# Spreading the last eight output transfers of an attention-and-convolution kernel over three issuing queues

## The chip, the cores and the metric

The kernel runs on one core of one Trainium2 chip. A core has five engines that run their own instruction streams: TensorE (PE in the profile) multiplies matrices into PSUM, VectorE (DVE) and ScalarE (ACT) do elementwise work, GpSimd (POOL) does slower elementwise work, and SyncE (SP) only issues transfers. The engines are held in order by semaphores. Transfers between the memory of the chip (HBM) and the on-core memory (SBUF) are issued by an instruction on SyncE, ScalarE or GpSimd and carried out by 16 DMA engines that all issuers share.

The metric is the device time of one execution in microseconds, lower is better. Before the change it is 220.62 us, the median of three runs that lie between 220.59 and 221.15 us.

## The reference

There are eight batches `b`, eight heads, 576 rows and 64 columns a head. A linear attention is followed by a gated long convolution:

```
kv  = einsum('bhsd,bhse->bhde', k, v)
out = einsum('bhsd,bhde->bhse', q, kv)
out = out / sqrt(mean(out*out, -1) + 1e-6) * g_norm
x   = out, heads side by side             # (8, 576, 512)
x1, x2, x3 = split(x @ w_proj, 3)
x2c = irfft(rfft(x2, axis=1) * rfft(filter, axis=0), axis=1)
y   = x1 * x2c * x3
return y @ w_out                          # (8, 576, 512), float32
```

The result has 9.4 MB and is written to HBM once.

## The kernel before

All work is cut into named steps, one function each, and three strings (`FIRST`, `ROUND`, `LAST`) write out by hand in which order the steps are given to the engines. `FIRST` fills the pipeline, `ROUND` is repeated seven times, each time with steps of several batches mixed, and `LAST` empties it. A step's name followed by plus or minus signs means the same step of a later or earlier batch. The Tile layer adds the semaphores and does not change the order. A step's instructions run as soon as their engine has reached them and the semaphores that they wait for are met.

A batch goes through loads by GpSimd (`L104`), the attention product and its norm, a Fourier transform written as matrix products, the gates (`L545`), the inverse transform (`L569`, `L570`), the product of the gates in `yg` (`L590`), and the last product with `w_out`. The 576 rows of a batch are held in an order of 18 blocks of 32 rows. The last product takes 128 rows at a time as one chunk; a chunk `c` has four blocks of 32, and two neighbouring chunks (0 and 1, or 2 and 3) form a pair. The 64 rows that are left over of two batches are put together in one step, `U4`.

For batches 0 to 6 a pair is one step: `U` (`L622`) multiplies, `U_ev` (`L626`) copies both chunks by ScalarE from PSUM to an SBUF tile and issues four transfers from SyncE (`L629`), each for 32 partitions and both chunks, 64 rows of 2 KB.

For the last batch the chunks are done one by one so that copies can start earlier. `V` (`L654`) multiplies one chunk, `V_ev` (`L659`) copies it by ScalarE (`va`) or VectorE (`vv`) to half of the pair's tile, and `V_out` (`L664`, steps `vd2` and `vd0`) issues the pair's four transfers, of the same 128 KB each, all from SyncE. The end of `LAST` reads

```
U4 V3 V2 vv3 ot4 V1 vv1 va2 vd2 V0 va0 vd0
```

so the pair of chunks 2 and 3 (its tile is named `o` in the trace) leaves with `vd2`, and the pair of chunks 0 and 1 (tile `rstd`) with `vd0`, which is the last work of the program. Both tiles reuse SBUF room of earlier steps. Between them stands `ot4` (`L639`, `L642`): the left-over rows of batches 6 and 7, four transfers of 64 KB; in this last batch alone they are issued from GpSimd.

Behind its last transfer SyncE waits for the landing of every transfer semaphore in use, two in one instruction, nine instructions in all (`L722`), and then all five engines meet at a barrier that ends the program. GpSimd has a drain of its own ahead of that barrier, behind its last transfer.

Of the kernel before, what the change touches and what calls it, by code (L numbers as in the profile page):

```python
# [39 lines left out]
def kernel(  # L40
# [11 lines left out]
    nc = tc.nc  # L52
# [22 lines left out]
    held, tmp = {}, {}  # L75
# [21 lines left out]
    def t_of(blk):  # L97
        return SB * (blk // 6) + blk % 6 // 3 + 2 * (blk % 3)
# [502 lines left out]
    def o_rows(b, *blks):  # L601
        t0 = [t_of(x) for x in blks]
        two = [[(t0[1] - t0[0]) * DM, 2]] if len(t0) == 2 else []
        return bass.AP(tensor=out.tensor, offset=out.offset + (b * S + t0[0]) * DM, ap=[[6 * DM, 32]] + two + [[1, DM]])
# [56 lines left out]

    def V_out(b, c0):
        for i in range(4):
            nc.sync.dma_start(out=o_rows(b, 4 * c0 + i, 4 * c0 + 4 + i), in_=tmp[c0 // 2][32 * i:32 * i + 32])  # L664

    for c in range(4):
        step["V%d" % c] = lambda b, c=c: V(b, c)
# [2 lines left out]
    for c0 in (0, 2):  # L670
        step["vd%d" % c0] = lambda b, c0=c0: V_out(b, c0)
# [55 lines left out]
```

## Time and profile before

| what | value |
|---|---|
| median of three runs | 220.62 us (220.59 to 221.15) |
| profiled execution | 221.07 us, of which the span of instructions is 219.3 us |
| PE, DVE, ACT, POOL busy | 94%, 87%, 68%, 23% of the span |
| granted TensorE clock | 0.998 |
| transfers through GpSimd's queue (q0) | 17.11 MB |
| transfers through SyncE's queue (q1) | 12.72 MB |
| transfers through a queue of ScalarE | none |

The profile page cuts the span into 40 slices of 5.5 us and gives each engine's busy share in tenths. A row of a group reads: line, engine, operation, tile written and tiles read, count, then durations. In a row of the timeline the first number is the start in us from the start of the span and the second the duration, and rows of one kind that follow each other are merged into one (x4). "SPq" is the instruction stream of SyncE; issuing does not count as busy, and the duration of a transfer row is the time that its issuer needed, not the time until the bytes arrived, which is given apart as "DMA to landing", from the start of the issue.

### The profile page before, as it was taken

The page shows a single profiled execution, that of the slowest core. Times are in us where ns is not written, and L with a number is a line of the kernel's source. Part 1 is how long each engine was busy: PE and PEld are TensorE (multiplying, and loading weights), DVE is VectorE, ACT ScalarE, POOL GpSimd, SP SyncE. Part 2 cuts the span into 40 slices and gives each one's busy share as a digit, 9 for nine tenths or more (in the row PEclk, how much of TensorE's full clock was granted, in tenths as well). Part 3 has the DMA queues.
Part 4 walks back from the last instruction along what each step waited for, and adds up shares of the span by engine and source line. Part 5 has one row for each costly group of instructions (what it writes and reads, how often), then busy time and mean ns, then how long its engine had stood idle before and what let it go on. Part 6 is the DMA issues. An engine that isn't in the chain of part 4 may idle for free.

```text
span 219.3 us, 4667 instructions
## 1 busy us (share of the span) xinstructions
PE 205.3 (94%) x1861; PEld 124.1 (57%) x1861; DVE 191.7 (87%) x323; ACT 148.6 (68%) x234; POOL 50.6 (23%) x55
## 2 busy tenths in 40 slices
PE   7599998999997999999999999999999999999970
PEld 2454635574575547754776477646774676467620
DVE  4977876899999989898989998989989999999930
ACT  3779876998954786678767785768685965542430
POOL 7843100406040206300450035000400050014030
PEclk9999999999999999999999999999999999999999
DMA  4999999988998599994969945909403211241376
GB/s 44 189 210 205 205 205 204 198 120 122 203 204 122 69 235 213 126 211 127 195 100 203 220 122 69 217 28 116 139 21 79 53 45 42 55 119 28 78 187 167
DMA packets 41064, 30.12 MB, mean 137 GB/s; under 512 B 15922, under 2 KB 36402, under 8 KB 41042
## 3 DMA queue, kind: packets, MB, share of 16 engines
q0 software_dynamic: 21200, 17.11, 51.4%
q1 hardware_dynamic: 19842, 12.72, 26.9%
q8 instruction: 14, 0.23, 0.4%
q14 instruction: 8, 0.07, 0.1%
HBM read 33.69 MB, written 9.44 MB: 197 GB/s over the span
## 4 chain that ended last, share of the span: by engine, by line
PE 74%; DMA 13%; DVE 4%; ACT 3%; issue 1%; POOL 1%; POOLq 0%; ACTq 0%
PE ps L545 23%; PE ps L622 10%; DMA kb<-in_k_dram 7%; PE ps L472 6%; PE ps L569 4%; DMA qb<-in_q_dram 3%; PE ps L321 3%; PE ps L458 3%; PE ps L479 3%; DMA qT<-qb 3%; PE ps L391 2%; PE ps L513 2%; PE ps L384 2%; PE ps L654 2%; PE ps L505 2%; PE ps L282 2%
## 5 line engine op out<-in xcount | busy, mean ns | idle before, releaser
L545 PE MATMUL ps<-x,wp 128*128 128x288 bf16 x512 | 70.4, 286 | 0.3 <-ACT x L483 0.3
L545 PEld LDWEIGHTS <-wp 128*128 128x128 bf16 x512 | 48.6, 98 | 15.3 <-issue 1.1
L526 POOL TENSOR_TENSOR Y<-tpw 97x1024 bf16<-97x1024 f32 x8 | 23.4, 2924 | 122.8 <-DVE tpw L520 85.6
L483 ACT CAST x<-ps 128x1024 bf16<-128x1024 f32 (+1 forms) x24 | 20.2, 872 | 15.5 <-PE ps L472 9.7
L405 ACT ACTIVATE rstd<-ps,bias_eps 128x576 bf16<-128x576 f32 x32 | 22.8, 740 | 6.1 <-PE ps L391 6.0
L622 PE MATMUL ps<-wo,yg 128*128 128x512 bf16 x112 | 26.5, 379 | 0.0
L551 ACT CAST x<-ps 128x576 bf16<-128x576 f32 x32 | 20.5, 643 | 7.2 <-PE ps L545 6.8
L553 DVE TENSOR_TENSOR g<-ps,x 128x576 bf16<-128x576 f32 x32 | 23.8, 750 | 0.8 <-PE ps L545 0.8
L394 ACT ACTIVATE sq<-ps 128x576 bf16<-128x576 f32 x32 | 20.3, 664 | 6.2 <-PE ps L384 5.9
L519 DVE TENSOR_TENSOR tpw<-ps,HH 97x1024 f32<-97x1024 f32 (+1 forms) x16 | 19.6, 1224 | 4.0 <-PE ps L506 2.6
L401 ACT ACTIVATE o<-ps,g_col 128x576 bf16<-128x576 f32 x28 | 20.4, 759 | 0.0
L520 DVE TENSOR_TENSOR tpw<-ps,HH 97x1024 f32<-97x1024 f32 (+1 forms) x16 | 19.4, 1215 | 0.0
L626 ACT COPY ot<-ps 128x1024 f32<-128x1024 f32 x13 | 13.3, 1021 | 8.9 <-PE ps L622 8.9
L622 PEld LDWEIGHTS <-yg 128*128 128x128 bf16 x112 | 10.6, 98 | 11.5
L569 PE MATMUL ps<-IV,Y 128*128 128x192 bf16 x128 | 16.5, 246 | 0.1
L472 PE MATMUL ps<-wp,ab 128*128 128x512 bf16 x64 | 15.1, 379 | 0.0
L573 ACT COPY os<-ps 128x576 f32<-128x576 f32 x16 | 10.3, 641 | 6.5 <-PE ps L570 6.5
L590 DVE TENSOR_TENSOR yg<-w,g 128x1152 bf16<-128x1152 bf16 x16 | 14.2, 886 | 0.0
L578 DVE TENSOR_TENSOR u<-ps,os 128x576 bf16<-128x576 f32 x16 | 12.0, 751 | 2.2 <-ACT os L573 2.2
L417 DVE TENSOR_TENSOR x<-o,rstd 128x1152 bf16<-128x1152 bf16 x16 | 11.9, 751 | 1.9 <-ACT rstd L405 1.9
L570 PE MATMUL ps<-IV,Y 97*128 97x96 bf16 x64 | 13.2, 207 | 0.0
L391 PE MATMUL ps<-sq,ind 128*128 128x288 bf16 x64 | 11.9, 286 | 0.3 <-ACT x L483 0.3
(138 smaller groups left out, 328.8 us busy)
## 6 DMA issues: line engine op xcount, KB each, us to landing
out_dram<-ot SPq DMA_DIRECT2D x52, 128.0 KB, 2.9
qb<-in_q_dram POOLq DMA_DIRECT2D x8, 576.0 KB, 8.6
kb<-in_k_dram POOLq DMA_DIRECT2D x7, 576.0 KB, 12.3
vb<-in_v_dram POOLq DMA_DIRECT2D x7, 576.0 KB, 8.8
wp<-in_moe_w_proj_dram POOLq DMA_DIRECT2D x3, 512.0 KB, 16.8
out_dram<-ot SPq DMA_DIRECT2D x12, 64.0 KB, 1.7
vb<-in_v_dram POOLq DMA_DIRECT2D x2, 288.0 KB, 7.3
kb<-in_k_dram POOLq DMA_DIRECT2D x2, 288.0 KB, 7.3
```

The source lines that it names most:

```text
L394: act.activation(out=halves(sq()[:, j]), in_=tmp['o', b, j][:, :, 0:TH], func=AF.Square)
L401: act.activation(out=by_time(osb(), j), in_=i_, func=AF.Copy, scale=g_col)
L405: act.activation(out=by_time(rstd(), j), in_=by_row(tmp['r', b, j]), func=AF.Abs_reciprocal_sqrt, scale=1.0 / D, bias=bias_eps)
L472: nc.tensor.matmul(pp[:, h], abt()[:, j, h * SB:h * SB + P], w2(j), start=(j == 0), stop=(j == NDC - 1))
L483: act.copy(out=o_(), in_=tmp[key, b])
L519: vec.tensor_mul(out=t_[:n, 0], in0=xp[:n], in1=HH[:n, g, 1:3])
L526: op(out=Yt()[:n, 2 * g:2 * g + 2], in0=t_[:n, :, 0], in1=t_[:n, :, 1])
L545: nc.tensor.matmul(pp[:, h, 0:TH], w_, x[:, j, h * TH:(h + 1) * TH], start=(j == 0), stop=(j == NDC - 1))
L551: act.copy(out=x1, in_=pp[:, :, 0:TH])
L553: vec.tensor_mul(out=halves(g13t()[:, dc]), in0=pp[:, :, 0:TH], in1=x1)
L569: nc.tensor.matmul(pp[:, i, 0:SB], Y[:, 2 * g + h, cs], IV[:, 2 * g + h, 0:SB], start=(g == 1), stop=(g == 2))
L622: nc.tensor.matmul(pp[:, cc], ygt(b)[:, dc, c * P:(c + 1) * P], wo[:, dc], start=(dc == 0), stop=(dc == NDC - 1))
```

## The change

`V_out` no longer issues all four transfers of a pair from SyncE. The first and the third stay there. The second and the fourth go to ScalarE for the pair of chunks 0 and 1 (`c0` is 0), and to GpSimd for the pair of chunks 2 and 3. The bytes, the shapes and the order of the steps stay as they are.

```
     def V_out(b, c0):
         for i in range(4):
-            nc.sync.dma_start(out=o_rows(b, 4 * c0 + i, 4 * c0 + 4 + i), in_=tmp[c0 // 2][32 * i:32 * i + 32])
+            (nc.sync if i % 2 == 0 else nc.gpsimd if c0 else nc.scalar).dma_start(
+                out=o_rows(b, 4 * c0 + i, 4 * c0 + 4 + i), in_=tmp[c0 // 2][32 * i:32 * i + 32])
```

## The prediction

> **What bounds the kernel now.** I read the page first, then the chain of waits, then the timeline of the last 10 us, then single transfers of line L664 in narrow windows.
>
> ```profile
> span 219.3 us, 4667 instructions
> PE   7599998999997999999999999999999999999970
> PEld 2454635574575547754776477646774676467620
> DMA  4999999988998599994969945909403211241376
> ```
>
> TensorE is full until slice 39 of 40; the last slice (from 213.8 us) has no TensorE work, only transfers. The change can act there alone: it issues the same bytes, and no instruction before the last batch's copies is touched.
>
> The chain of waits of the last ten microseconds, and the same stretch in the timeline:
>
> ```profile
> 209.63 3.58 PE ps L654 x16
> ...
> 213.22 0.59 ACT rstd L659
> ```
> ```profile
> 210.54 2.01 POOL L642 DMA_DIRECT2D out_dram<-ot  x4 [10.71 <-ACT ot L639]
> ...
> 211.50 0.59 ACT L659 COPY o<-ps 128x512 f32<-128x512 f32 x1 [1.25 <-PE ps L654]
> 212.11 1.73 SPq L664 DMA_DIRECT2D out_dram<-o  x4
> 212.36 0.69 DVE L659 COPY rstd<-ps 128x512 f32<-128x512 f32 x1 [1.03 <-PE ps L654]
> 213.22 0.59 ACT L659 COPY rstd<-ps 128x512 f32<-128x512 f32 x1 [1.14 <-PE ps L654]
> 213.95 2.33 SPq L664 DMA_DIRECT2D out_dram<-rstd  x4
> ```
>
> The last copy ends at 213.22 + 0.59 = 213.81 us. From there to the end of the span are 5.5 us: SyncE issues four transfers one behind the other, the last one lands, SyncE runs through its waits, the barrier ends the program. The single issues, each from its own narrow window:
>
> ```profile
> 212.11 0.32 SPq L664 DMA_DIRECT2D out_dram<-o  x1
> ...
> 213.42 0.43 SPq L664 DMA_DIRECT2D out_dram<-o  x1
> ...
> 213.95 0.58 SPq L664 DMA_DIRECT2D out_dram<-rstd  x1
> ...
> 214.57 0.60 SPq L664 DMA_DIRECT2D out_dram<-rstd  x1
> ...
> 215.22 0.59 SPq L664 DMA_DIRECT2D out_dram<-rstd  x1
> ...
> 215.85 0.43 SPq L664 DMA_DIRECT2D out_dram<-rstd  x1
> ```
>
> The four of the last pair stand 0.62 to 0.65 us apart, without a gap. The landings of the last one, and of all eight of L664, from the line's own view:
>
> ```profile
> L664 SPq DMA_DIRECT2D out_dram<-rstd x1: 434/434/434, 215.8 to 215.8; - x1
> DMA to landing us min/median/max: 2.2/2.2/2.2
> ```
> ```profile
> L664 SPq DMA_DIRECT2D out_dram<-rstd x4: 434/582/597, 214.0 to 215.8; - x4
> L664 SPq EVENT_SEMAPHORE  x2: 28/444/860, 210.5 to 213.9; - x2
> DMA to landing us min/median/max: 2.0/2.3/2.5
> ```
>
> So the last bytes land at 215.85 + 2.2 = 218.05 us. What follows is fixed: SyncE's waits (nine of the eleven rows) and the barrier. SyncE's first drain, behind the waits, is at 218.4:
>
> ```profile
> SPq L722 <- DMA out_dram<-rstd: 1.6, 3, 0.6
> ```
> ```profile
> L722 SPq EVENT_SEMAPHORE  x11: 17/28/28, 216.3 to 219.2; - x11
> L722 SPq DRAIN  x3: 7/7/13, 218.4 to 218.7; - x3
> ```
>
> 1.25 us lie between the last landing and the end of the span.
>
> **Is it issue or data that sets the pace?** The busy share of the DMA engines is 0.9 or more here, but that is no proof of a limit. The same kind of transfer (L629, 128 KB, 64 rows of 2 KB) was once queued behind a transpose; when it got the engines, the four moved at once:
>
> ```profile
> L629 SPq DMA_DIRECT2D out_dram<-ot x4: 437/448/525, 82.7 to 84.2; - x4
> DMA to landing us min/median/max: 4.2/4.4/4.6
> ```
> ```profile
> 85.00:86.50 1.50, 1.50 (x15) 1.18 (x13) 1.50 (x3) 1.11 (x2) 1.50 (x1) 1.00 1.08 365
> 213.00:217.50 4.50, 0.19 (x1) 0.00 (x0) 0.06 (x1) 0.59 (x1) 0.00 (x0) 1.00 0.91 244
> ```
>
> (The last number is GB/s, the one before it the DMA share.) At 365 GB/s 131 KB take 0.36 us; in the tail they come at 244, one per 0.54 us, which is the spacing of the issues (0.47 within the first pair, 0.62 to 0.65 within the second). The landings agree: first issue 82.7 + 4.6 = 87.3 at the latest reading, last 84.2 + 4.2 = 88.4, three steps in about 1 us. Hence the tail is set by how fast SyncE issues. The Trainium skill, "DMA: Bandwidth & Descriptors", section "Issuing engines are not separate DMA queues", says that issuing from several engines only saves the sequencer's time to start a transfer, usually small beside the transfer; by that rule there is little to win, but here the trace has issue as the larger of the two, 0.62 against 0.36.
>
> **The change part by part.**
>
> *SyncE, four issues fewer.* For `o` it issues two instead of four and is free at 212.11 + 0.32 + 0.04 + 0.43 = 212.90 instead of 213.85. Its next one no longer waits for SyncE (0.14 us lie between the end of the copy at 213.81 and 213.95, and only 0.02 between the copy's end at 211.50 + 0.59 = 212.09 and 212.11). So the first `rstd` transfer starts at about 213.83, the second 0.62 later at 214.45. Gain on SyncE's own queue: 215.85 - 214.45 = 1.40 us.
>
> *ScalarE, two issues more.* They stand behind ScalarE's last copy; nothing is queued behind them but the end. ScalarE issues no transfer in the trace, so the price is bounded. Below: no dearer than SyncE's first `rstd` issue, 0.58 and 0.04 of spacing. Above: SyncE's dearest issue of all, 1.92.
>
> ```profile
> L629 SPq DMA_DIRECT2D out_dram<-ot x52: 315/448/1922, 72.6 to 210.0; - x52
> ```
> ```profile
> 0.74 0.73 SPq L156 DMA_DIRECT2D g_col<-in_g_norm_dram  x1
> ```
>
> I take 0.73, SyncE's own first issue, since ScalarE's is a first one too (the 1.92 came in a stretch with other transfers under way). Second start: 213.83 + 0.73 + 0.04 = 214.60. With 2.3 to land (the median of the pair now) the last bytes are there at 216.9, against 218.05: 1.15 us earlier. With 1.92 for each of the two the second starts at 215.8 and, if what it costs over SyncE's 0.5 is added to its landing, the bytes are there at 215.8 + 2.3 + 1.4 = 219.5, a loss of 1.4. I stay near the lower end because ScalarE's queue is idle, as SyncE's was at 0.74. Eight transfers must then pass between 213.0 and 216.5, 1.05 MB in 3.5 us or 300 GB/s, under the 365 shown.
>
> *GpSimd, two issues more.* They stand behind its four of L642, free at 210.54 + 2.01 = 212.55. The nearest prices are its own 64 KB transfers (0.50 each) and the 576 KB loads (0.77):
>
> ```profile
> L642 POOL DMA_DIRECT2D out_dram<-ot x4: 498/505/539, 210.5 to 212.1; - x4
> DMA to landing us min/median/max: 2.0/2.0/2.3
> ```
> ```profile
> L104 POOL DMA_DIRECT2D vb<-in_v_dram x9: 672/772/794, 4.1 to 132.9; - x9
> ```
> ```profile
> L722 POOLq DRAIN  x1: 3224/3224/3224, 211.9 to 211.9; - x1
> ```
>
> The second starts between 213.05 and 213.3 and lands by 215.6 at 2.3 us. GpSimd's drain ends today at 211.9 + 3.2 = 215.1, 3.0 us after its last transfer began (about 212.1); so it would end at 216.1 to 216.3, still ahead of SyncE's waits at about 217.2. I cost this part at nothing; what hides it is the last pair, with 0.9 us to spare.
>
> *The end.* The transfers are spread anew over the eight landing semaphores that they share in turn. The new issues wait for earlier users of the same semaphore, the latest of which are SyncE's of L629 at 208.7 us and on, and GpSimd's loads, all landed before 212.4 (210.0 + 2.3): nothing.
>
> ```profile
> L629 SPq DMA_DIRECT2D out_dram<-ot x4: 316/428/433, 208.7 to 210.0; - x4
> DMA to landing us min/median/max: 1.9/2.2/2.3
> ```
>
> The waits at the end stay nine; ScalarE's second transfer is the fifth waited for, where the last one was fourth, one step of some 0.06 us less behind it.
>
> Sum: 1.15 + 0.06 = 1.2 us off. The profiled execution took 221.07 us, 0.45 above the median of 220.62; taken off its own time that is 219.9, and off the median 219.4 us. Its own range: landing at best 214.45 + 2.2, at worst 214.60 + 2.5, so 1.0 to 1.45 us off, 219.2 to 219.6.
>
> **The rivals.**
>
> *A: SyncE's and ScalarE's issues exclude each other.* If one unit makes the descriptors for both, the last four still follow each other at 0.62 to 0.65, now from 213.83 instead of 213.95: 0.1 us off, 220.5, no change. If they exclude each other for only half of the issue, half of the 1.2 is lost: 220.0. For it: no row shows two engines issuing at once. Against it, weakly: 64 KB on SyncE (L642, below) cost as much as the 128 KB ones at 0.43, so the time does not go into one row after another.
>
> ```profile
> L642 SPq DMA_DIRECT2D out_dram<-ot x4: 326/422/426, 147.3 to 148.6; - x4
> ```
>
> The Trainium skill, "Perfetto Trace Analysis", section "DMA Instruction — HWDGE (DVE, Sync)", has this rule: the block that generates descriptors is shared by two sequencers and locked by one at a time, and the wait for the lock is part of the profiled duration. By that rule ScalarE's rows would come out near 1.2 us, or in turn with SyncE's. No run here shows it yet.
>
> *B: data, not issue.* If the tail's 244 GB/s is what stores from these tiles can do, 1.05 MB still take 4.3 us from 213.0 and the end stays: 220.6. The row at 85.00 speaks against it.
>
> *C, slower: a cold ScalarE queue.* The place is ScalarE's first issue. The old end is reached when its two cost 2.5 us together (213.83 + 2.5 - 0.5 + 2.3 = 218.1), slower by over 0.66 us needs 3.2. At 1.92 each, 1.4 us are lost: 222.0. No row shows such a price on an idle queue, but no row shows the queue.
>
> **How the numbers follow.** 0.3% of 220.6 is 0.66 us, about what can be told from no change here. Forecast, with the half-way case of A that still saves over 0.66: 0.62. A: 0.22, B: 0.07, both within 0.3%. C: 0.09. Hence faster 0.62, same 0.29, slower 0.09. The range must take in A and B, so it reaches from 219.0, a little under the forecast's best, to 220.7; what is left out is C and a still shorter landing.
>
> **What would show it.** Right: ScalarE's two L664 rows start within 0.1 us of SyncE's two, last 0.58 to 0.75 each, the last landing is near 216.9 and the rate from 213 to 216.5 is near 300 GB/s. A shows as ScalarE and SyncE rows of double length or in turn. B shows as landings over 3 us after issue with all issues done by 215.2. C shows as one ScalarE row over 1.2. The step on GpSimd is wrong if its drain ends behind SyncE's waits. My surest wrong turn would be the price of ScalarE's issue, which has no row.

## The result, and the profile after

The changed kernel takes 220.25 us (median of 14 runs, 219.76 to 220.95) where the kernel before, in runs beside it, takes 221.03 us. The ratio is 0.9968 with a 95% interval of 0.9954 to 0.9983, about 0.7 us off. A second series gave 0.9975 (0.9957 to 0.9993), 0.55 us off. So the kernel became faster, by about half of the 1.2 us that were forecast. In the profiles of the tail, the only place where the change acts, the gain is smaller still, as the experiments show.

The page of the changed kernel differs little in its slices:

```profile
span 219.2 us, 4669 instructions
PE   7499998999998999999999999999999999999980
DMA  4999999988998599894969955918503211241375
```

The tail in the timeline. "ACTq" is the instruction stream of ScalarE, which now issues two transfers:

```profile
211.58 0.59 ACT L659 COPY o<-ps 128x512 f32<-128x512 f32 x1 [1.25 <-PE ps L654]
...
212.19 0.79 SPq L664 DMA_DIRECT2D out_dram<-o  x2
...
212.62 1.07 POOL L664 DMA_DIRECT2D out_dram<-o  x2
213.31 0.59 ACT L659 COPY rstd<-ps 128x512 f32<-128x512 f32 x1 [1.14 <-PE ps L654]
213.92 1.21 SPq L664 DMA_DIRECT2D out_dram<-rstd  x2
213.92 1.56 ACTq L664 DMA_DIRECT2D out_dram<-rstd  x2
```

The issues are where the prediction put them: the last of all starts at 214.7 us instead of 215.85. The landings are not. Line L664 in the window of the last pair, and SyncE's waits:

```profile
L664 SPq DMA_DIRECT2D out_dram<-rstd x2: 577/585/593, 213.9 to 214.5; - x2
L664 ACTq DMA_DIRECT2D out_dram<-rstd x2: 711/760/809, 213.9 to 214.7; - x2
DMA to landing us min/median/max: 3.1/3.3/3.5
```
```profile
SPq L723 <- DMA out_dram<-rstd: 2.5, 1, 2.5
```

Before, the same pair landed 2.2 to 2.35 us after its issue; now it takes 3.1 to 3.5. The last bytes are there at 214.675 + 3.34 = 218.01 us, and SyncE, which had nothing left to issue from 215.1, stands 2.5 us in one wait. To compare executions whose earlier part differs by some tenths, the times below count from the end of ScalarE's last copy (213.31 + 0.59 = 213.89 here, 213.81 before). From there the last landing came after 4.23 us before and after 4.12 us now, the end of the span after 5.46 and 5.29 us.

### The profile page after: what moved, and what is told of

The parts are those of the page before. It is cut to its first block, busy times and chain, and to the rows that moved or that the text cites. A ratio compares the mean times of both kernels' runs of the same rounds, so it can differ in the third digit from the quotient of the medians.

```text
span 219.2 us, 4669 instructions
## 1 busy us (share of the span) xinstructions
PE 204.9 (93%) x1861; PEld 124.3 (57%) x1861; DVE 191.7 (87%) x323; ACT 148.6 (68%) x234; POOL 51.7 (24%) x57
## 4 chain that ended last, share of the span: by engine, by line
PE 74%; DMA 13%; DVE 4%; ACT 3%; issue 1%; POOL 1%; POOLq 0%; ACTq 0%; DVEq 0%
PE ps L545 23%; PE ps L622 10%; DMA kb<-in_k_dram 7%; PE ps L472 6%; PE ps L569 4%; DMA qb<-in_q_dram 3%; PE ps L321 3%; PE ps L458 3%; PE ps L479 3%; DMA qT<-qb 2%; PE ps L391 2%; PE ps L513 2%; PE ps L384 2%; PE ps L654 2%; PE ps L505 2%; PE ps L282 2%
```

## Experiments

In this table "landing" is the last landing and "end" the end of the span, both in us from the end of ScalarE's last copy, worked out from starts, durations and landings in each trace. In two traces the transfer that came last has no landing; "about" marks them, and the time is when SyncE's wait for that transfer's semaphore ended. The kernels called "alone", "without" and "half the bytes" leave rows of the result unwritten. Ratios are to the kernel before in the same series.

| kernel | landing | end | ratio (95%) |
|---|---|---|---|
| before | 4.23 | 5.46 | |
| before, again | 4.33 | 5.55 | 1.0006 (0.9992 to 1.0021) |
| changed | 4.12 | 5.29 | 0.9968 (0.9954 to 0.9983) |
| changed, again | 4.21 | 5.41 | 0.9975 (0.9957 to 0.9993) |
| last pair SyncE and ScalarE, other pair SyncE | 5.49 | 6.72 | 1.0060 (1.0038 to 1.0083) |
| other pair SyncE and GpSimd, last pair SyncE | about 4.2 | 5.52 | 0.9996 (0.9981 to 1.0011) |
| last pair SyncE and GpSimd, other pair SyncE | about 4.5 | 5.97 | 1.0016 (0.9997 to 1.0035) |
| last pair all ScalarE, other pair SyncE | 5.56 | 6.79 | 1.0064 (1.0042 to 1.0086) |
| changed, without GpSimd's two | 3.88 | 5.04 | 0.9968 (0.9954 to 0.9981) |
| last pair alone, SyncE and ScalarE | 3.88 | 5.04 | 0.9966 (0.9952 to 0.9980) |
| last pair alone, SyncE and GpSimd | 3.94 | 5.55 | 0.9991 (0.9976 to 1.0007) |
| last pair alone, SyncE | 4.09 | 5.08 | 0.9989 (0.9978 to 1.0000) |
| changed, half the bytes in the last pair | 3.10 | 4.32 | 0.9944 (0.9926 to 0.9963) |
| all SyncE, new pairing | 4.00 | 5.23 | 0.9980 (0.9960 to 1.0000) |
| changed, new pairing | 4.00 | 5.20 | 0.9989 (0.9969 to 1.0010) |
| last pair alone, SyncE and ScalarE, new pairing | 3.68 | 4.84 | 0.9950 (0.9936 to 0.9964) |

### The two halves of the change, one at a time

The question was who holds the last pair up: SyncE and ScalarE each other (theory S), GpSimd's two transfers (G), or a ScalarE queue that is slow at first use (C). The cuts show what stands in place of the changed kernel's line that picks the issuer.

```
- (nc.sync if i % 2 == 0 else nc.gpsimd if c0 else nc.scalar).dma_start(
+ (nc.scalar if i % 2 and not c0 else nc.sync).dma_start(
```

> Only the last pair is split (SyncE and ScalarE in turns); the other pair stays on SyncE. Times from the end of ScalarE's last copy to the last landing (4.2 us before, 4.1 after the change). Theory S (SyncE's and ScalarE's transfers are served one after the other behind the issue, about 0.57 us each): still 4.0 to 4.2, time within 0.2 us of before. Theory G (GpSimd's two transfers, in flight at the same moment, hold up the last pair): without them the landings fall back to 2.3 us after issue, 3.1 from the copy, time 1.0 to 1.2 us under before. Theory C (ScalarE's queue is slow because it is used for the first time): as S, with SyncE's own two at 2.3 us and only ScalarE's late.

All theories missed: the kernel became 0.6% slower. The timeline, and the longest wait of this kind on SyncE:

```profile
213.72 1.34 ACTq L664 DMA_DIRECT2D out_dram<-rstd  x2
216.34 1.21 SPq L664 DMA_DIRECT2D out_dram<-rstd  x2
```
```profile
SPq L664 <- DMA out_dram<-rstd: 2.5, 1, 2.5
```

SyncE's first transfer of the last pair starts 2.6 us late. It waits for a landing semaphore that ScalarE's first transfer of the same pair has in use: the eight semaphores of SyncE's and ScalarE's transfers are dealt out in turn, and SyncE has two more transfers to cover here than in the change. In the change, GpSimd's two take semaphores of another set, and nobody meets. So the GpSimd part, worth nothing by itself (next run), is what keeps the ScalarE part from being a loss. The run is also a look at ScalarE's queue with no SyncE transfer of the last pair beside it: its two landed 2.55 and 2.20 us after issue. Theory C is out.

```
+ (nc.gpsimd if i % 2 and c0 else nc.sync).dma_start(
```

> Only the other pair is split (SyncE and GpSimd in turns); the last pair stays on SyncE, four issues. All theories give the last issue at about 215.8 on the old clock. S and C: landings at 2.2 to 2.35 us, time within 0.2 us of before. G: the first landings of the last pair rise to 2.6 us or more, the last one stays near 2.2 to 2.4 and the time is that of before or up to 0.2 us longer.

The time is that of before, 0.9996, and the last pair from SyncE alone lands in the old times although GpSimd's two are in flight as in the change:

```profile
213.96 2.32 SPq L664 DMA_DIRECT2D out_dram<-rstd  x4
```
```profile
DMA to landing us min/median/max: 2.2/2.4/2.4
```

G as the sole cause is out: the first transfer of SyncE, which landed after 2.36 us here, took 3.13 in the change, and of what was issued from the last copy on only ScalarE's two, in place of two of SyncE's, differ.

```
+ (nc.gpsimd if i % 2 and not c0 else nc.sync).dma_start(
```

> The last pair is split between SyncE and GpSimd, the other pair stays on SyncE, ScalarE issues nothing. S: GpSimd makes its own descriptors, so both halves go side by side: SyncE's last lands 2.3 us after its issue, GpSimd's last (issued some 0.55 us after its first) at 2.3 to 2.6, last landing 3.0 to 3.2 us after the copy, time 0.9 to 1.2 us under before. G: GpSimd's packets hold SyncE's up as in the changed kernel, landings of 3 us, 3.9 or more after the copy, time within 0.3 us of before. C: as S.

Nothing was gained, 1.0016. SyncE's first took 2.98 us to land, GpSimd's two 2.47 and 3.55. This spoke against S in its narrow form, with GpSimd in no way beside the others. Most of the loss is SyncE's second transfer of the pair, which has no landing in the trace: SyncE's wait for it lasted until 218.46, 4.5 us after the copy and 3.7 after its issue. On top of it comes a wait that I had costed at nothing, GpSimd's drain, which closes just behind SyncE's waits:

```profile
L723 POOLq DRAIN  x1: 4427/4427/4427, 214.7 to 214.7; - x1
L723 SPq DRAIN  x1: 13/13/13, 219.0 to 219.0; - x1
```
```profile
SPq L723 <- DMA out_dram<-rstd: 3.0, 1, 3.0
```

The drain ends at 214.7 + 4.4 = 219.1, about 0.1 us behind SyncE's.

```
+ (nc.sync if c0 else nc.scalar).dma_start(
```

> All four of the last pair from ScalarE, the other pair from SyncE. Issues of 0.71 to 0.81 us each: the last one starts 2.3 to 2.4 us after the copy. S: nothing of SyncE's is in the way any more (its last was issued 0.4 us before the copy's end), so ScalarE's land 2.3 us after issue, 4.7 after the copy, time 0.4 to 0.6 us over before. C: the first lands 3.3 us or more after issue, the later ones sooner. If ScalarE's transfers are slower at any time: all four land 3 us or more after issue, time 1 us or more over before.

ScalarE alone behaves like SyncE: issues of 0.71, 0.60, 0.60 and 0.44 us, last landing of the pair at 4.29 us, near SyncE's 4.23.

```profile
L664 ACTq DMA_DIRECT2D out_dram<-rstd x4: 437/602/710, 213.1 to 215.1; - x4
DMA to landing us min/median/max: 2.2/2.3/2.5
```

That confirms the end of C. The loss of 0.6% was the semaphores again: the last two transfers of the other pair on SyncE waited for a landing of ScalarE's, and the first of them started only 2.56 us after the copy.

```profile
SPq L664 <- DMA out_dram<-rstd: 3.5, 1, 3.5
```

### The changed kernel again, and with less around it

> The changed kernel unaltered, for a second profile and a second ratio. Its first profile has only 0.18 us less from the last copy to the end than before (5.29 against 5.46), while the runs are 0.7 us shorter. If the landings differ from execution to execution, this profile shows last-pair landings off 3.1 to 3.5 us by 0.3 us or more; if they are fixed, 3.1, 3.5, 3.1 and 3.3 come again and the ratio should come out nearer 0.999.

The landings came again, 3.1 to 3.8 us:

```profile
DMA to landing us min/median/max: 3.1/3.4/3.8
```

The gain in the runs came again too, 0.55 us, with 0.05 to 0.14 us in the tail.

> The changed kernel with GpSimd's two transfers of the other pair left out (64 partitions of its rows are not written); ScalarE and SyncE split the last pair as in the change, with the same landing semaphores. Theory S (transfers of SyncE and ScalarE in flight together are served one after the other): last-pair landings stay at 3.0 to 3.5 us, last landing 4.0 to 4.1 us after the copy. Theory G (GpSimd's packets cause it): landings of 2.2 to 2.5, last landing 3.0 to 3.2 us after the copy, time 1.0 us or more under before.

```
+            if c0 and i % 2:
+                continue
```

The last pair landed after 2.35 (SyncE's first), 3.16 and 3.10 us (ScalarE's), the last of them at 3.88. So GpSimd's two cost the changed kernel 0.24 to 0.33 us of landing, and the larger part of the delay stays without them. The 3.13 us of SyncE's first came from both together: it took 2.36 beside GpSimd's two alone and 2.35 beside ScalarE's two alone.

```
+            if c0:
+                continue
```

> The changed kernel with all four transfers of the other pair left out (its 128 partitions of rows are not written): the last pair's four, from SyncE and ScalarE, meet idle DMA engines. S: still 3.0 us or more for all but the first to be served, last landing 3.8 to 4.1 us after the copy. If it is the backlog of the other pair that holds them up (theory L): 2.2 to 2.5 us each, last landing 3.0 to 3.2 after the copy.

With idle DMA engines nothing changes against the run before: 3.88 us. Theory L is out. The line's view, and below it the same four transfers on SyncE alone:

```profile
L666 SPq DMA_DIRECT2D out_dram<-rstd x2: 576/580/585, 214.1 to 214.7; - x2
L666 ACTq DMA_DIRECT2D out_dram<-rstd x2: 705/719/733, 214.1 to 214.8; - x2
DMA to landing us min/median/max: 2.4/3.0/3.1
```

> The last pair's four transfers from SyncE alone, all four of the other pair left out (its rows are not written): one queue on idle DMA engines, beside 3.88 us (SyncE and ScalarE) and 3.94 us (SyncE and GpSimd) from the copy to the last landing with two. If transfers of different queues take turns, splitting gains little: SyncE's issues at 0.03, 0.65, 1.29 and 1.92 us, last landing 4.1 to 4.2. If splitting does overlap them, one queue should be far behind two: 4.4 or more.

```profile
L666 SPq DMA_DIRECT2D out_dram<-rstd x4: 426/582/595, 213.9 to 215.8; - x4
DMA to landing us min/median/max: 2.2/2.3/2.4
```

One queue: 4.09 us; two: 3.88. Issuing the last transfer 1.14 us earlier (0.78 instead of 1.92 after the copy) brought it home 0.21 us earlier. At the end of the span only 0.04 us of that are left (5.04 against 5.08): with one queue the last transfer has the semaphore that SyncE waits for eighth of nine, and 0.99 us follow its landing; with two it is the fifth, and 1.17 us follow.

> The last pair's four transfers from SyncE and GpSimd in turns, all four of the other pair left out (its rows are not written): the same as the last pair alone on SyncE and ScalarE (landings 2.35, 3.13, 2.88, 3.10 us after issue, last 3.88 after the copy), with GpSimd in ScalarE's place. Theory S (SyncE and ScalarE share one maker of descriptors that takes one transfer at a time, GpSimd has its own): SyncE's two land 2.3 us after issue, GpSimd's at 2.3 to 2.6, last landing 3.0 to 3.2 us after the copy. Theory Q (any two queues make way for each other at the DMA engines): landings of 2.9 us or more on both, last 3.7 or later.

```profile
L666 SPq DMA_DIRECT2D out_dram<-rstd x2: 576/580/585, 213.5 to 214.1; - x2
L666 POOL DMA_DIRECT2D out_dram<-rstd x2: 514/528/541, 213.7 to 214.2; - x2
DMA to landing us min/median/max: 2.4/3.0/3.1
```

With GpSimd as the second queue: 3.94 us, Q as expected but for SyncE's first (2.42 us), and S refuted in its narrow form. The packets of the DMA engines show what happens. Counted from the packet records of each trace, data packets that start in each 0.2 us, from 1.0 us after the copy (q1 is SyncE's queue, q10 ScalarE's, q0 GpSimd's; a transfer has 64 packets, on q0 32 of double size):

```
from, us           1.0 1.2 1.4 1.6 1.8 2.0 2.2 2.4 2.6 2.8 3.0 3.2 3.4 3.6
SyncE alone   q1     0  16  19  24  17  19  20  21  35  19  20  27  15   4
with ScalarE  q1     0  16  19  24   5   0   0   0  29  31   4   0   0   0
              q10    0   0   0   0  13  18  17  15   1   5  29  26   4   0
with GpSimd   q1     0  16  19  24   5   0   0   0  18  34  12   0   0   0
              q0     0   0   0   1  10   6  13   2   0   2  14  14   2   0
changed       q0    14   6   1   0   0   0   0   0   0   0   0   0   0   0
              q1     0   8  21  19  11   3   2   3  32  22   5   2   0   0
              q10    0   0   0   1   9  17  12  15   5  14  30  17   7   1
```

In these traces the first two transfers pass one after the other. The second one runs from 1.8 to 2.6 us whoever issues it, and whether that was at 0.03 us (ScalarE) or at 0.65 (SyncE alone). SyncE's own second transfer, issued at 0.65, does not start before 2.6, when the other queue's is through. Only the last transfer gains, as it follows the third at once. The order is not strict everywhere: in the second profile of the changed kernel, with half the bytes, and with the new pairing on two or three queues (below), packets of SyncE's and ScalarE's queues start side by side for half a microsecond and more.

What the traces do show is that the engines had little room left. The stretch in which the last pair alone passes, with two queues and with SyncE alone (the last two numbers are the share of the 16 DMA engines and GB/s):

```profile
215.20:217.60 2.40, 0.00 (x0) 0.00 (x0) 0.00 (x0) 0.00 (x0) 0.00 (x0) 0.60 0.87 219
```
```profile
215.10:217.70 2.60, 0.00 (x0) 0.00 (x0) 0.00 (x0) 0.00 (x0) 0.00 (x0) 1.00 0.85 202
```

With SyncE alone the engines already work 0.85 of 2.6 us, which is 2.2 us for the four transfers; unless a packet itself takes less time, splitting them over two queues can take off only the rest. A data packet of 2 KB takes 151 and 175 ns on average in the first two transfers of the two-queue run, 91 and 99 in the last two. By an even share each engine has four packets of a transfer, which gives 0.60, 0.70, 0.36 and 0.39 us, about the lengths of the turns.

### What a turn lasts

```
-            nc.sync.dma_start(out=o_rows(b, 4 * c0 + i, 4 * c0 + 4 + i), in_=tmp[c0 // 2][32 * i:32 * i + 32])
+            eng = nc.sync if i % 2 == 0 else nc.gpsimd if c0 else nc.scalar
+            if c0:
+                eng.dma_start(out=o_rows(b, 4 * c0 + i, 4 * c0 + 4 + i), in_=tmp[c0 // 2][32 * i:32 * i + 32])
+            else:
+                eng.dma_start(out=o_rows(b, 4 * c0 + i), in_=tmp[c0 // 2][32 * i:32 * i + 32, 0])
```

> The changed kernel with only the first of the two chunks in each transfer of the last pair (64 KB, 32 rows; the rows of chunk 1 are not written). If rows or bytes are what is served in turn: landings of the last pair fall by 0.3 us for the first and 0.8 to 1.0 us for the last, last landing about 3.2 us after the copy. If each transfer costs a fixed turn however short: no fall beyond 0.3 us, last landing 3.8 or later.

Landings fell to 2.4 to 2.6 us and the last one to 3.10, with 0.22 us from the first landing to the second (0.39 in the changed kernel, 0.79 in the last pair alone): the turn goes with rows or bytes. (The form changed with them, to 32 rows at one distance, and the issues fell to 0.33 to 0.43 us.) At 0.9944 it shows that a landing that does come a microsecond earlier shows in full, 1.1 us in the tail and 1.2 in the runs.

In the last pair alone, the first two turns took some 0.7 us and the last two 0.4 to 0.5. The first two have rows of a regular distance (form 64x1x512), the other two have not (32x2x512). Pairing chunk 0 with 2 and 1 with 3 gives all eight the second form:

```
+    PERM = (0, 2, 1, 3)
...
-                nc.tensor.matmul(pp, ygt(b)[:, dc, c * P:(c + 1) * P], wo[:, dc], start=(dc == 0), stop=(dc == NDC - 1))
+                nc.tensor.matmul(pp, ygt(b)[:, dc, PERM[c] * P:(PERM[c] + 1) * P], wo[:, dc], start=(dc == 0), stop=(dc == NDC - 1))
...
-                out=o_rows(b, 4 * c0 + i, 4 * c0 + 4 + i), in_=tmp[c0 // 2][32 * i:32 * i + 32])
+                out=o_rows(b, 4 * PERM[c0] + i, 4 * PERM[c0 + 1] + i), in_=tmp[c0 // 2][32 * i:32 * i + 32])
```

> The kernel before (all eight on SyncE), with the chunks of the last batch paired as 0 with 2 and 1 with 3 in place of 0 with 1 and 2 with 3, so that the two rows of a partition no longer lie three rows apart and all eight transfers have the form 32x2x512; the first two of the last pair had 64x1x512. If the maker's time goes by form (0.62 to 0.8 us for 64x1x512, 0.45 to 0.5 for 32x2x512): issues of the last pair 0.47 us apart, the first lands in 2.0 to 2.1 us, last landing 3.5 to 3.7 us after the copy against 4.23, time 0.5 to 0.7 us under before. If it goes by bytes alone: no change, within 0.2 us.

> The changed kernel (three queues) with the same new pairing of chunks. S with time by form: four turns of 0.45 to 0.5 us instead of two of 0.8 and two of 0.45, first landing 2.1 us, last landing 3.3 to 3.6 us after the copy against 4.1 to 4.2, time 1.0 to 1.3 us under before. Q or by bytes: last landing 4.0 or later, time as the changed kernel.

> Last pair alone on SyncE and ScalarE as in the run with 3.88 us, but with the new pairing of chunks (all four 32x2x512; the other pair is left out). If the turn goes with the form (0.75 to 0.8 us for 64x1x512, 0.45 for 32x2x512): first landing 2.0 to 2.1, then 0.45 each, last landing 3.2 to 3.5 us after the copy. If not: 3.8 or later, as with the old pairing.

On SyncE alone the four issues took 1.8 us instead of 2.3 and the last landing came at 4.00, less than half of what was expected; the ratio, 0.9980, touches 1. With three queues it is 4.00 as well and the ratio holds 1: the new pairing and the three queues do not add up. On idle engines the first landing fell to 2.05 us as expected, but the second came 0.73 us later all the same, and the last, at 3.68, lies between the two expectations. The first fence is from the kernel with all eight on SyncE, the second from the last pair alone:

```profile
214.28 1.81 SPq L666 DMA_DIRECT2D out_dram<-rstd  x4
```
```profile
L668 SPq DMA_DIRECT2D out_dram<-rstd x2: 316/372/427, 213.2 to 213.5; - x2
L668 ACTq DMA_DIRECT2D out_dram<-rstd x2: 393/414/435, 213.2 to 213.6; - x2
DMA to landing us min/median/max: 2.0/2.9/3.2
```

So the form sets the time of issue (0.32 to 0.43 against 0.58) and of the first landing, but not the length of the turn that changes queues: there a packet took 154 and 180 ns in the first two transfers, as with the old pairing. No kernel that writes the whole output beat the change clearly. The new pairing on SyncE alone cannot be told from it: 0.9980 against 0.9968 and 0.9975, with intervals that overlap, and a tail of 5.23 us against 5.29 and 5.41.

### The null comparison

> The kernel before, unaltered, as a null comparison and for a second profile. From the last copy to the end of the span its first profile has 5.46 us. If the tail differs between executions, this one differs from 5.46 by 0.2 us or more; if not, 5.4 to 5.5 and the last landing 4.2 us after the copy, and the ratio's interval holds 1.000.

The tail came again within 0.1 us (5.55 against 5.46), and the interval holds 1. The kernel before is stable in its tail; the changed kernel's two profiles (5.29, 5.41) are 0.05 to 0.26 us shorter, which is less than the 0.55 and 0.7 us of its runs. Both profiled executions of the changed kernel were the longest of their series (220.95 and 221.33 us, medians 220.25 and 220.33), but that does not make their tails long: executions differ in the part ahead of the tail. In the sixteen traces the last copy ends between 213.05 and 214.12 us, and the tail does not follow it: it lasts 5.04 us both where the copy ended at 213.15 (without GpSimd's two) and where it ended at 214.03 (last pair alone). So the medians of the runs carry a spread that the change cannot act on. The lower ends of the two intervals, 0.4 and 0.15 us, come near what the tail shows. Where the rest lies stays open.

## Why the prediction was right in its issues and wrong in its landings

- *SyncE's two issues fewer*: right. The second transfer of the last pair started at 214.54 us, 0.65 after the copy, forecast 0.64 (214.45 against a copy that ended at 213.81).
- *ScalarE's price*: right. 0.71 us for the first issue (forecast 0.73) and the second 0.78 after the copy (forecast 0.79). With it rival C fell: an idle ScalarE queue is as quick as SyncE's.
- *"With 2.3 to land the last bytes are there at 216.9"*: this is the term that failed. It took the landing time of one queue for two queues at once. Measured: 3.13 and 3.52 for the two first, 3.34 for the last, so 218.0, where 216.9 was forecast. Instead of 1.15 us the last landing came 0.02 to 0.21 us earlier (4.12 and 4.21 after the copy against 4.23 and 4.33). Of the delay some 0.8 to 0.9 us is there with two queues on idle engines too (3.10 for ScalarE's last, against 2.18 for SyncE's last when alone), and 0.24 to 0.33 is GpSimd's part. That the runs gained about half of the forecast is therefore no sign that half of the mechanism was right; what the tail does not explain of it is, as far as these runs show, luck.
- *"Is it issue or data that sets the pace?"*: the step before it, and where the error began ("the tail is set by how fast SyncE issues"). The 365 GB/s row was one queue with four transfers waiting in it, at 88 ns a packet of 2 KB; I read its 0.36 us a transfer as what the engines give anywhere. In the tail before the change the same packets took 122 ns on average, and the engines' share was 0.91. I had set that share aside as no proof of a limit, but 0.91 of 4.5 us is 4.1 us of work for the engines, and I asked for as much in 3.5. My sign, near 300 GB/s from 213 to 216.5, did not come: 239, where it had been 246 before. Over the longer window two queues gave 247 as before's 244. Both rows of the changed kernel:

```profile
213.00:216.50 3.50, 0.27 (x2) 0.00 (x0) 0.14 (x1) 0.59 (x1) 0.70 (x2) 0.99 0.84 239
213.00:217.50 4.50, 0.27 (x2) 0.00 (x0) 0.14 (x1) 0.59 (x1) 0.70 (x2) 0.88 0.83 247
```

- *GpSimd's two, costed at nothing*: half right. They started in the forecast window (213.16), but landed after 2.82 and 2.95 us instead of 2.3, at 216.1, and the drain ended at 213.0 + 3.9 = 216.9 instead of 216.1 to 216.3; SyncE's waits ended at 218.3, so it cost nothing there. Beside the last pair they cost 0.24 to 0.33 us, which I had not counted.

```profile
L723 POOLq DRAIN  x1: 3917/3917/3917, 213.0 to 213.0; - x1
```

- *The semaphores*: right for this kernel, by a margin that I did not see: without GpSimd's two the same ScalarE half is 0.6% slower.
- *Rival A* had the effect (each transfer behind the other) but not the sign that I gave for it: the issue rows are not in turn and not doubled. It is behind the issue. The rule quoted for it, from the Trainium skill's "Perfetto Trace Analysis", section "DMA Instruction — HWDGE (DVE, Sync)", would put the wait into the issue rows, and these hardly grew: SyncE's stayed at 0.58 and 0.59, ScalarE's first took 0.71, as it does with no SyncE issue beside it (0.71 in two runs), and its second 0.81 instead of 0.59 and 0.60 there; and by that page's section "DMA Instruction — SWDGE (GPSIMD)" GpSimd does not use the shared block, yet it waited its turn alike (3.94 against 3.88 us). The measurement decides: a block shared by SyncE and ScalarE is not enough to explain it. What I gave for A, that no row shows two engines issuing at once, was a wrong reading: in my own timeline GpSimd's L642 lasts until 212.55 and SyncE's L664 starts at 212.11. No row showed it for SyncE and ScalarE.
- *Rival B*, that data set the pace, is the one whose sign came: landings over 3 us after issue (3.13 to 3.52), with the last issue begun at 214.7 and over at 215.5 (the sign had 215.2), and a rate that did not rise. The row at 85.00, which I held against it, does not refute it, as the same packets took less time there. Why a packet takes longer in the tail (82 to 248 ns, where nearly all took 84 in the middle of that row) no run shows, so it stays open whether the data, or the making of the transfers, is what holds the engines.

The Trainium skill's "DMA: Bandwidth & Descriptors", section "Rules for kernel authors", says that two transfers from disjoint halves of the partitions serialize, as both are spread over the same DMA engines. The runs agree: 3.88 and 3.94 us with two queues, 4.09 with one. I had weighed the neighbouring rule, on issue time, and set it aside because issue seemed the larger term, 0.62 against 0.36; in the tail, at 122 ns a packet, it was 0.62 against about 0.5 (four packets an engine, an estimate from the packet records), and 0.21 us were all that it was worth.

So the step that failed is known, and the cause behind it only in part. What makes the first two transfers of two queues pass by turns of 0.7 us, when their packets could be mixed, and why their packets take 150 to 180 ns where those of the last two take 91 to 99, is not settled by these runs.

## What to carry to other kernels

Before splitting a row of transfers over issuers, look at the share of the DMA engines in that stretch: here it was 0.91 already, and a rate read in another stretch (365 GB/s) did not hold. Price the split by a transfer's landing with another queue in flight, not by its landing alone and not by the issue time saved: here 1.14 us of earlier issue gave 0.21 us of earlier landing. Look also at which landing semaphores the new issuer shares; moving two transfers to ScalarE cost 0.6% as soon as SyncE's next one needed a semaphore that ScalarE held. And count the drain of GpSimd at the end: it closes 0.75 to 0.83 us behind GpSimd's last landing, so the last transfers of a program are better kept off it.

## What was not expected of the hardware

- The first two transfers of different queues pass one after the other even on idle engines, with GpSimd as with ScalarE as the second queue. The second transfer's packets start from 1.8 to 2.6 us after the copy in all three traces of the last pair alone, issued at 0.03, 0.29 or 0.65 us.
- The same 2 KB packet of a store took 84 ns in one stretch and 150 to 180 on average in another, with the 16 engines busy in both; a rate read in one stretch does not hold in the other.
- GpSimd's drain follows its last landing, not its last issue: 215.09 against a landing at 214.34 before, 216.94 against 216.11 after, 0.83 behind also with the last pair on it (3.94 and 4.77 us after the copy).
- A transfer whose rows lie at one regular distance (64x1x512) took SyncE 0.58 us to issue and 2.35 to land; the same bytes as 32x2x512 took 0.32 and 2.03 in the same place.
